# Expert stage of a fused attention and mixture-of-experts kernel: next unit's weights loaded ahead of row gathers, static weights moved to another queue, output tiles of their own

## The chip, the cores and the metric

The kernel runs on one core of one Trainium2 chip. The metric is the device time of one execution in microseconds (us). Three runs of the kernel before gave 756.05, 757.34 and 758.69 us, the median is 757.34 us. Engines are named as in the profile: PE (TensorE), PEld (its weight loads), DVE (VectorE), ACT (ScalarE), POOL (GpSimd) and SP (SyncE, which only issues DMAs here).

## What is computed

```
attn = clustered attention of q, k, v            # 2 x 8 heads x 768 x 64
x    = prelu(attn @ w_in) @ w_out                # 1536 tokens x 512, hidden 2048
do   = (x @ w_skip) > 0                          # tokens that go to an expert
e    = argmax(x @ w_gate, 8 experts)
gate = softmax(x @ w_gate)[e]
out  = x;  out[do] = x + gate * (relu(x @ w1[e]) @ w2[e])    # w1 512 x 1024, w2 1024 x 512
```

The change is in the last stage, the experts, and in the routing just ahead of it.

## The kernel before

The order of the instructions on each engine is written out by hand (a manual schedule). Attention and the dense layer fill the first 540 us. What follows is the expert stage, `moe2` (L1166), with the end of the routing, `route_last` (L1025), woven in.

**Units and tiles.** The stage has ten units, `TURNS = "01U2UZUVWV"`. A unit is one expert's weights and one or two tiles of tokens: units 0, 1 and 3 (the letters "0", "1", "2") have an expert that is known when the kernel is built, the others one that the routing picks. The sixteen tiles are t0 to t15: unit 0 has t0 and t1, unit 1 has t2, unit 2 has t3 and t4, unit 3 has t5, unit 4 has t6 and t7, unit 5 t8, unit 6 t9 and t10, unit 7 t11 and t12, unit 8 t13, unit 9 t14 and t15.

**Weights.** A unit's weights come in four chunks (c = 0 to 3) of 128x2048 float32, 1 MB each. `loadw(n, c)` (L1180) loads chunk c of unit n into a landing buffer, `raw` for odd units, `even` for even ones: for a unit with a picked expert by an indirect DMA that POOL issues (L1186) with row numbers `wi`, for a static one by a plain DMA from SP (L1184). `ahead()` in `run` then splits a chunk into a rounded high part, `wsp.hi` on ACT (L1432), and a low part, `wsp.lo` on DVE (L1436), and calls `loadw(n + 2, c)`. PE multiplies by both parts.

**Tiles.** `gather(t)` (L1174) is an indirect DMA from POOL that brings 128 token rows (L1163), with row numbers `gi`; `transx` turns them on PE, `first` is the first product, `transh` turns its result, `second` is the second product, `output(t)` (L1266) adds the gated result to the gathered rows `x` in place (DVE, L1278), and `scatter(t)` (L1281) writes them with an indirect DMA from POOL (L1283). A tile of x is kept in one of seven buffers, `XG = (1, 6)`, so `gather(t + 7)`, which stands right behind `scatter(t)` in the program, writes the buffer that `scatter(t)` reads. Each scatter waits for the one before it, since all write the same output.

**Routing.** `route_last` is a generator that `begin` (L1286) steps through between products. It makes `gi` from the product `sv` (L1118), `wi` and `si` from the product `eu` (L1135), and ends with the number of units, `nt`. Its tiles lie in a pool (`rwk`) that is closed after its end; the six buffers for gathered rows from t3 on (`moxg`) take that place.

**Queues.** POOL issues gathers, indirect weight loads and scatters in program order, and an instruction that waits holds all behind it. SP has a queue of its own.

Of the kernel before, what the change touches and what calls it, by code (L numbers as in the profile page):

```python
# [8 lines left out]
F32 = mybir.dt.float32  # L9
# [7 lines left out]
ALU = mybir.AluOpType  # L17
# [3 lines left out]
P = 128  # L21
# [5 lines left out]
DM = H * D  # L27
BIG = float(2 ** 60)
DFF = 2048
NE = 8  # L30
DE = 1024
NTT = N // P
NPC = 4
# [51 lines left out]
XG = (1, 6)  # L85
# [932 lines left out]
def route_last(nc, A, cst, R, wk, ps, yb, y1d):  # L1018
# [20 lines left out]
    s = wk.tile([P, KD, P], F32, tag="yts", name="yts")  # L1039
# [23 lines left out]
    def small(*shape):  # L1063
        return wk.tile([P, *shape], F32, name=f"rs{len(sizes)}", tag=f"rs{sizes.append(0) or len(sizes)}")
    sizes = []
    tm, cmp, m, nu, rem, n4, lim = small(NE), small(NE, 28), small(NE), small(NE), small(NE), small(4), small(3, 4)
    dist, far, bl, tri = small(3), small(3, NE), small(NE), small(4, NE, NE + 1)
    mt, sl4, ta, tb, sl = small(NTT, 4, NE), small(NTT, 4), small(NTT), small(NTT), small(NTT)
    tt, red = ve.tensor_tensor, ve.tensor_reduce
    steps = [  # L1070
        lambda: tt(out=tm, in0=rk[:, nt], in1=R["one8"][:, 1], op=ALU.max),
# [26 lines left out]
    more = positions(nc, R, wk, rk[:, :nt], t0, nt)  # L1098
# [18 lines left out]
    for i in range(NTT):  # L1117
# [5 lines left out]
    t2 = wk.tile([P, NTT, nx], F16, tag="t2", name="t2")  # L1123
    tt(out=t2, in0=sl.unsqueeze(2).to_broadcast([P, NTT, nx]),
       in1=R["first"].unsqueeze(1).to_broadcast([P, NTT, nx]), op=ALU.is_equal)
    es = wk.tile([P, NTT, NE], F32, tag="es", name="es")
    e0 = wk.tile([P, NTT], F32, tag="e0", name="e0")
    ve.tensor_tensor(out=es, in0=M, in1=R["e512"].unsqueeze(1).to_broadcast([P, NTT, NE]), op=ALU.mult)
    ve.tensor_reduce(out=e0, in_=es, axis=AX.X, op=ALU.add)
# [33 lines left out]
    nc.gpsimd.indirect_dma_start(out=x, out_offset=None, in_=y1d, in_offset=bass.IndirectOffsetOnAxis(ap=at, axis=0))  # L1163


def moe2(ctx, tc, A, cst, R, y1d, wsp, wk, ps, x0, route, room):  # L1166
    nc = tc.nc
    ident = cst["ident"]
    KD = DM // P
# [4 lines left out]
    def gather(t):  # L1174

        a, b = XG
        x = (wk if (t - 2) % (a + b) < a else more[0]).tile([P, DM + 1], F32, tag="xg", name="xg", bufs=a if (t - 2) % (a + b) < a else b)
        gather_rows(nc, x, y1d, R["gi"][:, t:t + 1])
        xg[t] = x

    def loadw(n, c):
        if n not in TOLD:
            r = (EXPERT[int(TURNS[n])] * NPC + c) * P
            nc.sync.dma_start(out=wsp.src(n, c), in_=A["wall"][r:r + P])  # L1184
            return
        nc.gpsimd.indirect_dma_start(out=wsp.src(n, c), out_offset=None, in_=A["wall"],  # L1186
                                     in_offset=bass.IndirectOffsetOnAxis(ap=R["wi"][:, TOLD[n], c:c + 1], axis=0),
                                     bounds_check=NE * NPC * P - 1, oob_is_err=False)
# [75 lines left out]
        scatter(t, output(t))  # L1264

    def output(t):  # L1266
        x = xg.pop(t)
        n, b0, nr = TILES[t]

        rows = slice(0, b0 + nr)  # L1270
        y = yo.pop(t)
        if is_half(t):
            o = wk.tile([P, DM], F32, tag="o", name="o", bufs=1)
            for r in range(b0, -1, -HALF):
                nc.scalar.copy(o[r:r + HALF], y[HALF - r:P - r])
            nc.vector.tensor_tensor(out=o[rows], in0=y[rows], in1=o[rows], op=ALU.add)
            y = o
        nc.vector.scalar_tensor_tensor(out=x[rows, :DM], in0=y[rows], scalar=x[rows, DM:DM + 1], in1=x[rows, :DM], op0=ALU.mult, op1=ALU.add)  # L1278
        return x

    def scatter(t, o):  # L1281
        rows = slice(0, TILES[t][1] + TILES[t][2])
        nc.gpsimd.indirect_dma_start(out=A["out"], out_offset=bass.IndirectOffsetOnAxis(ap=R["si"][rows, t:t + 1], axis=0), in_=o[rows, :DM], in_offset=None,  # L1283
                                     bounds_check=N - 1, oob_is_err=False)

    def begin():  # L1286

        low = []
        next(route)
        first(0, 0, range(0, 1))  # L1290
        wsp.take(1, 0)
        wsp.hi(1, 0)
        next(route)
        first(0, 0, range(1, 4))
        next(route)
        first(1, 0)
        transh(0, 0, low)
        first(0, 1)
        transh(1, 0, low)
        first(1, 1)  # L1300
        transh(0, 1, low)
        second(0, 0, (0,))
        next(route)
        gather(2)
        next(route)
        second(0, 0, (1,))
        wsp.take(1, 1)
        wsp.hi(1, 1)
        while low:
            low.pop(0)()  # L1310
        second(0, 1, (0,))
        next(route)
        transh(1, 1)
        for _ in route:
            pass
        more.append(room())
        for t in (3, 4):
            gather(t)
        for c in range(NPC):
            loadw(2, c)  # L1320
        second(0, 1, (1,))
        second(0, 0, (2,))
        wsp.lo(1, 0, nc.vector)
        wsp.take(1, 2)
        wsp.hi(1, 2)
        transx(2)
        second(0, 1, (2,))
        second(1, 0)
        wsp.lo(1, 1, nc.vector)
        scatter(0, output(0))  # L1330
        second(1, 1)
        wsp.lo(1, 2, nc.vector)
        scatter(1, output(1))
        for c in range(3):
            loadw(3, c)
        for t in range(5, sum(XG) + 2):
            gather(t)

    def run(n0, n1, fresh=False):

# [99 lines left out]
def kernel(ctx, tc, A):  # L1440
    nc = tc.nc
# [25 lines left out]
    R = {}  # L1467
# [177 lines left out]
    xg, (y, xT) = got  # L1645
    c3.close()
    c0.close()
    c4 = ctx.enter_context(ExitStack())
    rwk = c4.enter_context(tc.tile_pool(name="rwk", bufs=1, side="right", reuse_waits="tile"))
    yb = rwk.tile([P, DM], F32, name="yb")  # L1650
# [14 lines left out]
        c4.close()  # L1665
        return ctx.enter_context(tc.tile_pool(name="moxg", bufs=1, side="right", reuse_waits="tile"))

    moe2(ctx, tc, A, cst, R, y1d, wsp, mwk, ps, (xg, xT), route_last(nc, A, cst, R, rwk, ps, yb, y1d), room)


# [45 lines left out]
```

## Time and profile before

| | |
|---|---|
| median of 3 runs | 757.34 us (756.05 to 758.69) |
| the profiled execution's own time | 755.56 us |
| its span in the profile | 753.8 us |
| mean granted clock of PE in it | 0.978 |
| busy PE / PEld | 713.6 us (95%) / 628.3 us (83%) |
| busy DVE / ACT / POOL | 568.2 us (75%) / 477.7 us (63%) / 363.6 us (48%) |
| DMA | 109.22 MB, mean 145 GB/s |

Busy shares are means over the whole span; stages differ. In a row of the timeline the columns are: start in us from the span's start, duration in us, engine, line of the kernel, operation, output<-inputs, how many instructions were merged, and in brackets the idle time of that engine just before with what ended it ("issue": nothing that the profile shows). The time of the profiled execution stands 1.78 us under the median.

### The profile page before, as it was taken

How to read it: one execution, taken by the hardware profiler on the slowest of the kernel's cores; microseconds unless marked ns; L12 is line 12 of the kernel's file. 1: busy time of each engine (PE TensorE's matmuls, PEld its weight loads, DVE VectorE, ACT ScalarE, POOL GpSimd, SP SyncE). 2: the span in 40 equal slices, each digit the busy share in tenths (PEclk: the TensorE clock that was granted, in tenths of full speed). 3: DMA queues.
4: the chain of work that ended last, by engine and by line, in shares of the span. 5: the costliest groups of instructions: out<-in, count | busy, mean ns of one | idle time of the engine just before them, and what ended most of it. 6: DMA issues, size and time to landing. Idle time of an engine off the chain costs nothing. (4 is left out here: it accounts for less than half of the span.)

```text
span 753.8 us, 11621 instructions
## 1 busy us (share of the span) xinstructions
PE 713.6 (95%) x4022; PEld 628.3 (83%) x4022; DVE 568.2 (75%) x1110; ACT 477.7 (63%) x916; POOL 363.6 (48%) x336
## 2 busy tenths in 40 slices
PE   8999999999999999999999999999986999987993
PEld 5988998889998889888899999988875888876772
DVE  5989988898989788888759899764785677755641
ACT  5879889798899845554446555565445675645630
POOL 4649779788785576666640000010271565534311
PEclk8999999999999999999999999999996999999997
DMA  7867668574763324333126000355366674646600
GB/s 205 223 163 179 129 137 212 125 184 99 210 137 96 113 65 150 122 113 111 57 98 196 0 1 1 68 185 172 109 234 275 223 283 160 258 161 250 244 26 25
DMA packets 46161, 109.22 MB, mean 145 GB/s; under 512 B 10778, under 2 KB 26586, under 8 KB 40720
## 3 DMA queue, kind: packets, MB, share of 16 engines
q1 hardware_dynamic: 39600, 72.01, 34.7%
q0 software_dynamic: 6496, 36.40, 13.3%
q8 instruction: 34, 0.56, 0.3%
q14 instruction: 31, 0.25, 0.1%
HBM read 74.78 MB, written 10.10 MB: 113 GB/s over the span
## 5 line engine op out<-in xcount | busy, mean ns | idle before, releaser
L341 DVE TENSOR_TENSOR etl<-pt,eth 128x384 fp32r<-128x384 f32 x192 | 102.1, 550 | 20.5 <-ACT eth L340 18.9
L1163 POOL DMA_INDIRECT xg<-y1d,gi x16 | 22.9, 1430 | 176.7 <-DVE gi L1014 113.8
L340 ACT CAST eth<-pt 128x384 fp32r<-128x384 f32 x192 | 91.1, 487 | 20.4 <-PE pt L338 20.3
L338 PE MATMUL pt<-ident,e 128*128 128x128 f32 x576 | 93.8, 272 | 0.3 <-ACT e L327 0.3
L320 DVE TENSOR_REDUCE nm<-s 128x1 f32<-128x768 f32 x96 | 90.5, 944 | 4.0 <-PE s L307 3.8
L327 ACT ACTIVATE e<-s,nm 128x768 f32<-128x768 f32 x96 | 87.5, 911 | 5.8 <-DVE nm L320 5.1
L695 ACT CAST gh<-gm 128x384 fp32r<-128x384 f32 x60 | 30.8, 514 | 82.0 <-DVE gm L693 58.5
L338 PEld LDWEIGHTS pt<-ident,e 128*128 128x128 f32 x576 | 73.5, 140 | 7.1 <-ACT e L327 0.5
L697 DVE TENSOR_TENSOR gl<-gm,gh 128x384 fp32r<-128x384 f32 x60 | 49.4, 823 | 25.7 <-ACT gh L695 25.7
L1436 DVE TENSOR_TENSOR wl<-raw,wh 128x2048 fp32r<-128x2048 f32 (+2 forms) x27 | 46.6, 1735 | 28.9 <-ACT wh L1432 28.4
L356 PE MATMUL px<-etl,vh 128*64 128x384 f32 (+1 forms) x192 | 65.6, 369 | 1.7 <-DVE etl L341 1.5
L304 PE MATMUL s<-AB 128*128 128x384 f32 x192 | 57.6, 381 | 2.6 <-ACT e L327 2.0
L1432 ACT CAST wh<-raw 128x2048 fp32r<-128x2048 f32 (+2 forms) x27 | 39.3, 1462 | 27.5 <-DMA raw<-in_wall_dram,wi 20.0
L667 PE MATMUL h<-xh,wh 128*128 128x384 f32 x256 | 55.6, 338 | 0.6 <-DVE gm L690 0.4
L667 PE MATMUL h<-xh,wl 128*128 128x384 f32 x256 | 56.0, 340 | 0.0
L667 PE MATMUL h<-xl,wh 128*128 128x384 f32 x256 | 55.0, 336 | 0.0
L567 POOL TENSOR_TENSOR pre<-ct,pre 128x512 int32<-128x512 int32 x26 | 37.1, 1448 | 35.9 <-DVE ct L565 35.9
L358 PE MATMUL px<-eth,vh 128*128 128x384 f32 x160 | 54.0, 337 | 0.0
L307 PE MATMUL s<-CD 128*128 128x384 f32 x192 | 49.4, 338 | 0.9 <-DMA CD<-st 0.9
L667 PEld LDWEIGHTS h<-xh,wh 128*128 128x128 f32 x256 | 45.6, 188 | 3.3 <-DVE gm L690 0.5
L1283 POOL DMA_INDIRECT out_dram<-xg,si x16 | 20.8, 1302 | 54.0 <-issue 27.1
L667 PEld LDWEIGHTS h<-xh,wl 128*128 128x128 f32 x256 | 44.6, 188 | 2.7 <-POOL wl L639 2.6
(343 smaller groups left out, 1844.3 us busy)
## 6 DMA issues: line engine op xcount, KB each, us to landing
AB<-RL SPq DMA_DIRECT2D x32, 384.0 KB, 5.2
raw<-in_wall_dram SPq DMA_DIRECT2D x12, 1024.0 KB, 8.9
raw<-in_w_in_dram SPq DMA_DIRECT2D x16, 512.0 KB, 4.0
raw<-in_w_out_dram SPq DMA_DIRECT2D x16, 512.0 KB, 4.7
Tp<-in_qkT_dram SPq DMA_DIRECT2D x16, 384.0 KB, 3.8
CD<-RL SPq DMA_DIRECT2D x16, 384.0 KB, 6.6
vt<-in_v_dram SPq DMA_DIRECT2D x8, 384.0 KB, 6.2
y1d<-yb SPq DMA_DIRECT2D x12, 256.0 KB, 4.5
```

Of the source, the lines that this page charges most:

```text
L304: nc.tensor.matmul(s[:, u, :384], lhsT=AB[:, 0, t * P:(t + 1) * P], rhs=AB[:, 1, ks], start=True, stop=False)
L307: nc.tensor.matmul(s[:, u, :384], lhsT=CD[:, 0, t * P:(t + 1) * P], rhs=CD[:, 1, ks], start=False, stop=True)
L320: nc.vector.tensor_reduce(out=nm, in_=s[:, :, :384], axis=AX.XY, op=ALU.max, negate=True)
L327: nc.scalar.activation(e.rearrange("p (u c) -> p u c", u=2), s[:, :, :384], AF.Exp, bias=nm, accum_out=den[:, i % 3:i % 3 + 1])
L338: nc.tensor.transpose(pt[:, i2], e[:, kt * P:(kt + 1) * P], ident)
L340: nc.scalar.copy(eh, pt)
L341: lows[u] = lambda: nc.vector.tensor_tensor(out=etl[:, 3 * u:3 * u + 3, q * P:(q + 1) * P], in0=pt, in1=eh.bitcast(F32), op=ALU.subtract)
L356: nc.tensor.matmul(px[:m], lhsT=vh[:, kt, :m], rhs=etl[:, kt], start=False, stop=False)
L358: nc.tensor.matmul(px, lhsT=vh[:, kt, :], rhs=eth[:, kt], start=False, stop=(kt == NT - 1))
L667: nc.tensor.matmul(hs[c], lhsT=a[:, k * P:(k + 1) * P], rhs=x[:, k, c * HC:(c + 1) * HC], start=(k == 0 and i == 0), stop=(k == KD - 1 and ...
L697: eng.tensor_tensor(out=gl[:, o], in0=m, in1=gh[:, o].bitcast(F32), op=ALU.subtract)
L1436: eng.tensor_tensor(out=lo[:, a:b], in0=self.src(t, c)[:, a:b], in1=hi[:, a:b].bitcast(F32), op=ALU.subtract)
```

## The change

It makes five edits.

1. In `begin`, the loads of unit 2's chunks 0 and 1 are issued as soon as `wi` is there, ahead of the gathers of t3 and t4; chunks 2 and 3 follow after the gather of t3, and the gather of t4 comes behind them.
2. The static loads that `loadw` makes, the four chunks of unit 3, are issued by POOL and no longer by SP, and three of them are placed behind the gathers of t5 to t8; the fourth follows in `run`.
3. `output` writes into a tile of its own, `o` (two buffers in a new pool `moo`), which `scatter` reads; before it wrote into `x`. The pool also takes the one gather buffer that lay in `mowk`.
4. The step of `route_last` that makes `sv` and `gi` is called two groups of matmuls sooner.
5. Two temporaries of the routing (`mt`, `es`) take the room of a tile that is no longer read.

```diff
-    mt, sl4, ta, tb, sl = small(NTT, 4, NE), small(NTT, 4), small(NTT), small(NTT), small(NTT)
+    room = s.rearrange("p k m -> p (k m)")
+    mt = room[:, :NTT * 4 * NE].rearrange("p (t c e) -> p t c e", t=NTT, c=4)
+    sl4, ta, tb, sl = small(NTT, 4), small(NTT), small(NTT), small(NTT)
...
     def loadw(n, c):
         if n not in TOLD:
             r = (EXPERT[int(TURNS[n])] * NPC + c) * P
-            nc.sync.dma_start(out=wsp.src(n, c), in_=A["wall"][r:r + P])
+            nc.gpsimd.dma_start(out=wsp.src(n, c), in_=A["wall"][r:r + P])
             return
...
     def output(t):
+        o = op.tile([P, DM], F32, tag="o", name="o")
         x = xg.pop(t)
...
         if is_half(t):
-            o = wk.tile([P, DM], F32, tag="o", name="o", bufs=1)
             for r in range(b0, -1, -HALF):
...
-        nc.vector.scalar_tensor_tensor(out=x[rows, :DM], in0=y[rows], scalar=x[rows, DM:DM + 1], in1=x[rows, :DM], op0=ALU.mult, op1=ALU.add)
-        return x
+        nc.vector.scalar_tensor_tensor(out=o[rows], in0=y[rows], scalar=x[rows, DM:DM + 1], in1=x[rows, :DM], op0=ALU.mult, op1=ALU.add)
+        return o
...
         first(1, 1)
+        next(route)
         transh(0, 1, low)
         second(0, 0, (0,))
-        next(route)
         gather(2)
...
         transh(1, 1)
+        for c in range(2):
+            loadw(2, c)
         for _ in route:
             pass
         more.append(room())
-        for t in (3, 4):
-            gather(t)
-        for c in range(NPC):
-            loadw(2, c)
+        gather(3)
...
         transx(2)
+        for c in range(2, NPC):
+            loadw(2, c)
+        gather(4)
...
         scatter(1, output(1))
+        for t in range(5, sum(XG) + 2):
+            gather(t)
         for c in range(3):
             loadw(3, c)
-        for t in range(5, sum(XG) + 2):
-            gather(t)
...
+    mop = ctx.enter_context(tc.tile_pool(name="moo", bufs=2, side="right", reuse_waits="tile"))
```

POOL's queue at the start of the expert stage, before. `xg<-` are gathers, `even<-` the four chunks of unit 2, then of unit 4, `out_dram<-` scatters; the first row is routing.

```order
L1000 TENSOR_SCALAR poh<-iota,pos,tok_5478 128x128 x6
L1163 DMA xg<-y1d,gi 128x513 x3
L1186 DMA even_5272<-in_wall_dram,wi 128x2048
L1186 DMA even_6291<-in_wall_dram,wi 128x2048
L1186 DMA even_6539<-in_wall_dram,wi 128x2048
L1186 DMA even_6540<-in_wall_dram,wi 128x2048
L1283 DMA out_dram<-xg_3831,si 1536x512
L1283 DMA out_dram<-xg_3832,si 1536x512
L1163 DMA xg<-y1d,gi 128x513 x4
L1186 DMA even_5272<-in_wall_dram,wi 128x2048
```

The same place in the change; `raw<-in_wall_dram` without `wi` are the four static chunks of unit 3.

```order
L1165 DMA xg<-y1d,gi 128x513
L1188 DMA even_5272<-in_wall_dram,wi 128x2048
L1188 DMA even_6291<-in_wall_dram,wi 128x2048
L1165 DMA xg<-y1d,gi 128x513
L1188 DMA even_6542<-in_wall_dram,wi 128x2048
L1188 DMA even_6543<-in_wall_dram,wi 128x2048
L1165 DMA xg<-y1d,gi 128x513
L1285 DMA out_dram<-o,si 1536x512 x2
L1165 DMA xg<-y1d,gi 128x513 x4
L1186 DMA raw_78<-in_wall_dram 128x2048
L1186 DMA raw_79<-in_wall_dram 128x2048
L1186 DMA raw_3822<-in_wall_dram 128x2048
```

Unit 2's first two chunks moved from the fourth and fifth DMA of the stage to the second and third; t4's gather moved from third to sixth; four loads joined the queue behind the gathers of t5 to t8.

POOL's queue around the scatters of t2 to t4 and the gathers behind them, before, with what each waits for (DMASW: an earlier DMA of POOL's queue, DMAHW: one of SP's).

```order
L1283 DMA out_dram<-xg,si 1536x512 [waits DMASW2_49,DVE_49]
L1163 DMA xg<-y1d,gi 128x513 [waits DMASW3_49,DMASW2_49,PE_49]
L1186 DMA even_6540<-in_wall_dram,wi 128x2048 [waits DMASW4_49,DVE_49]
L1186 DMA raw_78<-in_wall_dram,wi 128x2048 [waits DMAHW3_49,DMASW5_49,DVE_49]
L1186 DMA raw_79<-in_wall_dram,wi 128x2048 [waits DMAHW4_49,DMASW6_49,DVE_49]
L1186 DMA even_5272<-in_wall_dram,wi 128x2048 [waits DMASW7_49,DVE_49]
L1186 DMA raw_3822<-in_wall_dram,wi 128x2048 [waits DMAHW5_49,DMASW0_49,DVE_49]
L1283 DMA out_dram<-xg,si 1536x512 [waits DMASW1_49,DVE_49]
L1163 DMA xg<-y1d,gi 128x513 [waits DMASW1_49,PE_49]
L1283 DMA out_dram<-xg,si 1536x512 [waits DMASW3_49,DVE_49]
L1163 DMA xg<-y1d,gi 128x513 [waits DMASW4_49,DMASW3_49,PE_49]
```

The same place in the change.

```order
L1285 DMA out_dram<-o,si 1536x512 [waits DMASW6_49,DVE_49,Activation_49]
L1165 DMA xg<-y1d,gi 128x513 [waits DMASW7_49,PE_49]
L1188 DMA even_6543<-in_wall_dram,wi 128x2048 [waits DMASW0_49,DVE_49]
L1188 DMA raw_78<-in_wall_dram,wi 128x2048 [waits DMASW1_49,DVE_49]
L1188 DMA raw_79<-in_wall_dram,wi 128x2048 [waits DMASW2_49,DVE_49]
L1188 DMA even_5272<-in_wall_dram,wi 128x2048 [waits DMASW3_49,DVE_49]
L1188 DMA raw_3822<-in_wall_dram,wi 128x2048 [waits DMASW4_49,DVE_49]
L1285 DMA out_dram<-o,si 1536x512 [waits DMASW6_49,DMASW5_49,DVE_49]
L1165 DMA xg<-y1d,gi 128x513 [waits PE_49]
L1285 DMA out_dram<-o,si 1536x512 [waits DMASW7_49,DMASW5_49,DVE_49]
L1165 DMA xg<-y1d,gi 128x513 [waits DMASW0_49,PE_49]
```

The order is the same; a gather behind a scatter waited for that scatter's DMA (DMASW2, DMASW1, DMASW3) and no longer does, while the second of two scatters still waits for the first.

DVE's output additions of t9 and t10 and what stands behind them, before.

```order
L1436 TENSOR_TENSOR wl_6290<-even_6540,wh_6289 128x2048 [waits DMASW6_49,Activation_49]
L1278 SCALAR_TENSOR_TENSOR xg<-yo,xg 128x512 [waits PE_49] x2
L1436 TENSOR_TENSOR lastl<-raw_78,lasth 128x2048 [waits DMASW7_49,Activation_49]
L1248 TENSOR_TENSOR hTl<-pt,hTh 128x512 [waits Activation_49]
L1436 TENSOR_TENSOR wl_5614<-raw_79,wh_5613 128x2048 [waits DMASW0_49,Activation_49]
```

The same place in the change.

```order
L1440 TENSOR_TENSOR wl_6290<-even_6543,wh_6289 128x2048 [waits DMASW2_49,Activation_49]
L1280 SCALAR_TENSOR_TENSOR o<-yo,xg 128x512 [waits DMASW6_49,DVE_49,PE_49]
L1280 SCALAR_TENSOR_TENSOR o<-yo,xg 128x512 [waits DMASW1_49,DVE_49,PE_49]
L1440 TENSOR_TENSOR lastl<-raw_78,lasth 128x2048 [waits DMASW3_49,Activation_49]
L1250 TENSOR_TENSOR hTl<-pt,hTh 128x512 [waits Activation_49]
```

The additions now wait for the scatter of two tiles earlier (DMASW6, DMASW1), whose buffer they write; the low parts of weights and activations stand behind them.

## Rows read from the trace of the kernel before

**Rows 1.** Busy time by stretch, all engines: stretch, length, busy time (instructions), PEclk, DMA share, GB/s.
```profile
565.00:570.00 5.00, 0.00 (x0) 0.00 (x0) 1.11 (x1) 3.04 (x4) 0.18 (x1) 0.73 1.01 428
575.00:580.00 5.00, 4.07 (x14) 3.40 (x14) 2.38 (x3) 2.17 (x2) 0.04 (x1) 0.50 0.47 188
...
620.00:640.00 20.00, 20.00 (x96) 16.40 (x95) 15.34 (x12) 11.79 (x13) 10.64 (x7) 1.00 0.49 171
...
680.00:700.00 20.00, 15.85 (x77) 13.14 (x77) 10.23 (x9) 9.61 (x11) 8.89 (x9) 0.91 0.72 276
```

**Rows 2.** Timeline, PE, around unit 1's end and in unit 2.
```profile
562.31 0.61 PE L1150 MATMUL pt<-ident,xg 128*128 128x128 f32 x4
571.57 2.07 PE L1195 MATMUL yo<-wh,hTh 128*128 128x512 f32 x4 [8.65 <-DVE hTh L1245]
...
590.08 0.60 PE L1240 MATMUL pt<-ident,hb 128*128 128x128 f32 x4
```

**Rows 3.** Timeline, ACT, the same stretch.
```profile
561.03 0.58 ACT L1151 CAST xTh<-pt 128x512 fp32r<-128x512 f32 x1
566.96 1.90 ACT L1432 CAST lasth<-even 128x2048 fp32r<-128x2048 f32 x1 [5.35 <-DMA even<-in_wall_dram,wi]
...
587.10 0.60 ACT L1224 ACTIVATE hb<-h 128x512 f32<-128x512 f32 x1 [0.21 <-PE h L1195]
...
597.87 1.91 ACT L1432 CAST wh<-even 128x2048 fp32r<-128x2048 f32 x1 [2.95 <-DMA even<-in_wall_dram,wi]
```

**Rows 4.** Timeline, POOL, the same stretch: gather, weight load, two scatters, weight load.
```profile
552.35 2.48 POOL L1163 DMA_INDIRECT xg<-y1d,gi  x1 [2.37 <-DVE nt L1145]
555.13 2.31 POOL L1186 DMA_INDIRECT even<-in_wall_dram,wi  x1 [0.30 <-issue]
...
564.15 1.02 POOL L1283 DMA_INDIRECT out_dram<-xg,si  x1 [0.31 <-issue]
579.96 2.40 POOL L1283 DMA_INDIRECT out_dram<-xg,si  x1 [14.78 <-issue]
...
590.33 2.88 POOL L1186 DMA_INDIRECT even<-in_wall_dram,wi  x1 [0.30 <-issue]
```

**Rows 5.** Timeline, SP's queue, the four static loads of unit 3.
```profile
554.07 9.27 SPq L1184 DMA_DIRECT2D raw<-in_wall_dram  x4
```

**Rows 6.** Timeline, DVE, the same stretch: wi, then low parts of weights.
```profile
549.95 0.22 DVE L1138 TENSOR_TENSOR wi<-et,prow 128x64 uint32<-128x64 f32 x1
...
551.71 2.29 DVE L1436 TENSOR_TENSOR wl<-raw,wh 128x2048 fp32r<-128x2048 f32 x1
...
560.71 2.28 DVE L1436 TENSOR_TENSOR wl<-raw,wh 128x2048 fp32r<-128x2048 f32 x1
...
568.89 2.29 DVE L1436 TENSOR_TENSOR lastl<-even,lasth 128x2048 fp32r<-128x2048 f32 x1 [5.29 <-ACT lasth L1432]
```

**Rows 7.** Timeline, PE, its gaps between 655 and 705 us and two pairs of transposes.
```profile
661.41 0.66 PE L1240 MATMUL pt<-ident,hb 128*128 128x128 f32 x4 [2.28 <-ACT hb L1224]
...
664.66 0.60 PE L1240 MATMUL pt<-ident,hb 128*128 128x128 f32 x4
...
666.17 0.66 PE L1157 MATMUL pt<-ident,xg 128*128 128x128 f32 x4 [0.47 <-DVE hTl L1248]
...
687.09 1.12 PE L1240 MATMUL pt<-ident,hb 128*128 128x128 f32 x4 [4.15 <-ACT hb L1224]
...
691.80 1.00 PE L1236 MATMUL pt<-two,hb 128*128 128x64 f32 x8
...
704.76 1.20 PE L1195 MATMUL yo<-wh,hTh 128*128 128x512 f32 x4 [0.87 <-DVE hTh L1245]
```

**Rows 8.** Timeline, ACT, its longest wait in that stretch.
```profile
682.84 1.90 ACT L1432 CAST wh<-raw 128x2048 fp32r<-128x2048 f32 x1 [12.21 <-DMA raw<-in_wall_dram,wi]
```

**Rows 9.** Timeline, POOL, a gather behind a scatter, and the load that ACT waited for.
```profile
668.49 0.98 POOL L1163 DMA_INDIRECT xg<-y1d,gi  x1 [8.35 <-DMA out_dram<-xg,si]
...
677.00 1.01 POOL L1186 DMA_INDIRECT raw<-in_wall_dram,wi  x1 [0.30 <-issue]
```

More of the change, by code (lines that the diff above doesn't have):

```diff
@@ L1125, in route_last @@
        in1=R["first"].unsqueeze(1).to_broadcast([P, NTT, nx]), op=ALU.is_equal)
-    es = wk.tile([P, NTT, NE], F32, tag="es", name="es")
+    es = room[:, NTT * 4 * NE:NTT * 5 * NE].rearrange("p (t e) -> p t e", t=NTT)
     e0 = wk.tile([P, NTT], F32, tag="e0", name="e0")
@@ L1163, in gather_rows, with moe2 @@
     nc.gpsimd.indirect_dma_start(out=x, out_offset=None, in_=y1d, in_offset=bass.IndirectOffsetOnAxis(ap=at, axis=0))
-def moe2(ctx, tc, A, cst, R, y1d, wsp, wk, ps, x0, route, room):
+def moe2(ctx, tc, A, cst, R, y1d, wsp, wk, op, ps, x0, route, room):
     nc = tc.nc
@@ L1176, in gather @@
         a, b = XG
-        x = (wk if (t - 2) % (a + b) < a else more[0]).tile([P, DM + 1], F32, tag="xg", name="xg", bufs=a if (t - 2) % (a + b) < a else b)
+        x = (op if (t - 2) % (a + b) < a else more[0]).tile([P, DM + 1], F32, tag="xg", name="xg", bufs=a if (t - 2) % (a + b) < a else b)
         gather_rows(nc, x, y1d, R["gi"][:, t:t + 1])
@@ L1277, in output @@
             y = o
-        nc.vector.scalar_tensor_tensor(out=x[rows, :DM], in0=y[rows], scalar=x[rows, DM:DM + 1], in1=x[rows, :DM], op0=ALU.mult, op1=ALU.add)
-        return x
+        nc.vector.scalar_tensor_tensor(out=o[rows], in0=y[rows], scalar=x[rows, DM:DM + 1], in1=x[rows, :DM], op0=ALU.mult, op1=ALU.add)
+        return o
     def scatter(t, o):
         rows = slice(0, TILES[t][1] + TILES[t][2])
-        nc.gpsimd.indirect_dma_start(out=A["out"], out_offset=bass.IndirectOffsetOnAxis(ap=R["si"][rows, t:t + 1], axis=0), in_=o[rows, :DM], in_offset=None,
+        nc.gpsimd.indirect_dma_start(out=A["out"], out_offset=bass.IndirectOffsetOnAxis(ap=R["si"][rows, t:t + 1], axis=0), in_=o[rows], in_offset=None,
                                      bounds_check=N - 1, oob_is_err=False)
@@ L1666, in room @@
         return ctx.enter_context(tc.tile_pool(name="moxg", bufs=1, side="right", reuse_waits="tile"))
-    moe2(ctx, tc, A, cst, R, y1d, wsp, mwk, ps, (xg, xT), route_last(nc, A, cst, R, rwk, ps, yb, y1d), room)
+    moe2(ctx, tc, A, cst, R, y1d, wsp, mwk, mop, ps, (xg, xT), route_last(nc, A, cst, R, rwk, ps, yb, y1d), room)
 _OUTS = [((N, DM), 'float32')]
```

## The prediction

> **What bounds the kernel now.** I read the page first (PE busy 95% of the span), then busy time by stretch, then PE's timeline where it was idle, and from there the timelines of whoever it waited for. In the expert stage PE is the bound wherever its input is there: 20.00 of 20 us from 620 to 640, but nothing from 565 to 570 and 15.85 of 20 from 680 to 700 [rows 1]. So time can come from PE's gaps and from what the granted clock does around them, and from nothing else.
>
> There are two sets of gaps. The first is 8.65 us up to 571.57 [rows 2]. Its chain: PE waits for a low part of activations on DVE, which stands behind the low part of a weight chunk (568.89) [rows 6], which waits for ACT's cast of that chunk at 566.96, and the cast waited 5.35 us for the DMA [rows 3]. The chunk is unit 2's first, issued at 555.13 [rows 4], so it took 11.8 us to land. In that time the DMA engines were full (share 1.01, 428 GB/s from 565 to 570 [rows 1]): SP had started unit 3's four static megabytes at 554.07 [rows 5], which nobody needs yet. The granted clock fell in the gap (0.73 over 565 to 570, then 0.50, the lower of the two levels, 1.2 of 2.4 GHz) and was still 0.50 from 575 to 580 [rows 1].
>
> The second set is 2.28, 0.47, 4.15 and 0.87 us between 661 and 705, 7.77 us in all [rows 7]. They are one story: weights come late because POOL issues them late. ACT waited 12.21 us for a chunk [rows 8] that POOL issued only at 677.00, after gathers had held its queue; the gather at 668.49 sat 8.35 us until the scatter's DMA released its buffer [rows 9]. Five gathers in the stage wait like that, 7 to 9 us each.
>
> **The change part by part.**
>
> *Routing product sooner.* The same matmuls in another order, in a stretch where PE was not idle: 0 us, between a loss of 0.6 (one transposition, if PE must now wait for DVE) and a gain of nothing, since t2's rows were not waited for. The moved temporaries change no duration: 0.
>
> *Unit 2's chunks first.* `wi` is ready at 550.17 [rows 6]. An issue takes 1.02 us and 0.30 between two; beside a low part of weights on DVE it takes more, 2.48 for the one at 552.35, which ended 0.83 us after the low part that ran until 554.00 [rows 4, 6]. Landing comes 4.7 us after an issue's end (593.21 to 597.87) [rows 3, 4]. Chunk 0 is therefore issued at about 550.5 and lands at 556, far ahead of 561.6, when ACT is free for it (561.03 + 0.58) [rows 3]. The cast ends at 563.5, the low part runs from 563.6 to 565.9, and PE could go on 2.68 us after that start, as before (568.89 to 571.57), at 566.3 instead of 571.57 [rows 2, 6].
>
> *But t4's gather is late.* It is now sixth in POOL's queue. Ahead of it four DMAs pass beside the low parts that DVE runs from 551.71 to 562.99 [rows 6], so it is issued by 561.5 to 564 and lands 4.7 us later, at 566.2 to 568.7. PE transposes it (0.61, at 562.31 before [rows 2]) ahead of the product that ends the gap. PE goes on at 566.8 to 569.3; I take 567.5, a gap of 4.6 us.
>
> *Static loads behind thirteen other DMAs.* This takes back most of that gain. The scatter of t1 waits for that of t0: 14.78 us before, behind full DMA engines [rows 4]; now less is queued, and I put it at 567.5 (t0's scatter issued at 562 to 564, its data landing no later than 4.7 us after). Before, from that scatter to the first load behind the four gathers took 10.37 us (579.96 to 590.33) and the landing another 7.54 (to 597.87) [rows 3, 4]. The same pattern puts unit 3's first chunk in place at 585.4. ACT's cast of it (1.90) stands ahead of the `hb` of t4 (0.60, at 587.10 before [rows 3]), which PE transposes at 590.08 [rows 2]. PE would get there at 583.5: from 567.5, the 18.5 us of before (571.57 to 590.08) less some 2.5 for matmuls no longer at 0.50 (an estimate; PE was busy 4.07 of 5 us at that clock in one stretch of the two [rows 1]). The chunk lets it go on at 585.4 + 1.90 + 0.60 = 587.9. So a gap of 4.4 us opens, and what is left of the 8.65 is 590.08 - 587.9 = **2.2 us**. A plain load issued by POOL has no row; I price it as an indirect one of the same size. If t1's scatter goes at 566.9 and all issues are undisturbed, the chunk lands at 579.2, PE never waits and 7.3 us are gained; if the scatter goes at 570.5, the chunk lands at 588.4 and 0.8 us are lost.
>
> *The clock.* After the 2.28 us gap the three groups up to the next transposition took 3.25 us (661.41 to 664.66), after the 4.15 us gap 4.71 (687.09 to 691.80) [rows 7], where the granted clock was 0.91 over the stretch [rows 1]: 1.46 us more. I take that loss for a gap of 4.4: **-1.46**. A like loss after the earlier gap would fall into the wait for the chunk and cost nothing.
>
> *Outputs in tiles of their own.* Same DVE instructions, same sizes. The gather behind a scatter waits for DVE's addition alone, long past, so the five waits of 7 to 9 us leave POOL's queue, and what comes next is DVE's low part of the chunk whose buffer a load reuses. Unit 7's chunks are then issued some 20 us sooner than they were (an estimate, from two to three such waits); they were late by at most 12.21 [rows 8]. The whole second set goes, with the clock loss after it: **7.77 + 1.46 = 9.2 us**; nothing if POOL stays as late as now. What is late next is nothing: PE's work from 655 to 705 is what it was full with from 620 to 640. Against that the additions wait for the scatter two tiles earlier (third rival).
>
> *Sum:* 2.2 - 1.46 + 9.2 = 10.0 us. The profiled execution took 755.56 us (span 753.8) and becomes 745.6; it stands 1.8 under the median, so the median goes from 757.34 to **747.3 us**.
>
> **The rivals.**
>
> *Unit 3's chunks come in time* (17%). Then 7.3 + 9.2 = 16.5 us, 740.8 us. For it: several of POOL's issues may miss the low parts and take 1.02. Against: before, in the like stretch, most met one.
>
> *The second set of gaps stays, in part or whole* (12%). A second scatter of a unit still waits for the first, and loads stand behind both: 14.78 us was one such wait [rows 4]. With half the 9.2 the median is 752.0 us; with none 756.6, no change.
>
> *Two output buffers, full queue: slower* (8%). All of POOL's DMAs now share one queue. Before t2's scatter stand seven chunks. At 428 GB/s [rows 1] one takes 2.45 us, so from 583 they end at about 600 and the scatter lands at 602; t4's addition, which needs that buffer, comes near 604. The margin is under 2 us. If a plain load from POOL moves at half that rate, unit 3's second chunk is 4.9 us late and the scatter 9.8; DVE then stands some 8 us with low parts behind it, of which 4 to 5 reach PE, and again at t5: 2.2 - 4.9 - 1.46 - 9 + 9.2 = -4 us, 761 us. It decides from about one and a half times 2.45 us a chunk. The Trainium skill has a rule that speaks for this rival: DMA: Bandwidth & Descriptors, section SWDGE vs HWDGE vs iDMA, sends plain transfers to SP or ACT and leaves GpSimd the irregular ones, since GpSimd's descriptors are written by software and VectorE can lock it out while it does so. The lengthened issue at 552.35 agrees with the lock; that a chunk moves more slowly for it no row shows, and the one landing behind a 2.88 us issue speaks against [rows 3, 4].
>
> **How the numbers follow.** The forecast has 55% (745 to 750.5, by where the chunk lands), the rivals 17, 12 and 8, the remaining 8% small mixtures of them. The range 740.5 to 753.5 us takes in the first rival and half of the second, and leaves out the third. About 0.3% (2.3 us) is what a measurement of this kernel can tell from no change. Faster by more than that: 55 + 17 + some 6 of the second rival + 7 = 85%; within it 7%; slower 8%.
>
> **What would show it.** Right: unit 2's first chunk landed before ACT asks; PE's first gap down to 4 or 5 us, ended by a gather or by DVE; a new gap of 3 to 6 us in unit 2, ended by `hb`, with ACT waiting for a `raw` load without `wi`; POOL's gathers behind scatters without waits; no PE gap from a late chunk after 600. Wrong: if the new gap is missing (first rival), if ACT still waits for indirect `raw` loads in units 7 to 9 (second), or if additions on DVE or copies on ACT wait for scatters (third).

## The result and the profile after

| | before | after |
|---|---|---|
| median, measured side by side | 756.11 us (754.07 to 758.69) | 742.95 us (742.39 to 743.77) |
| the profiled execution's own time | 755.56 us | 742.98 us |
| its span | 753.8 us | 741.2 us |
| busy PE | 713.6 us (95%) | 711.5 us (96%) |

The ratio is 0.9825, 95% interval 0.9805 to 0.9845: faster by 13.2 us where 10.0 were forecast. PE runs the same 4022 matmul instructions; of the 12.6 us that the span lost, 10.5 are PE's idle time and 2.1 its busy time (the mean granted clock is 0.985 where it was 0.978).

The second set of gaps [rows 7] is gone. Busy time by stretch in the changed kernel (columns as in rows 1):

```profile
560.00:565.00 5.00, 4.16 (x15) 3.48 (x16) 4.31 (x4) 3.39 (x5) 3.03 (x2) 0.66 0.95 377
565.00:570.00 5.00, 4.08 (x27) 3.48 (x26) 2.67 (x4) 3.25 (x5) 1.73 (x2) 1.00 0.12 48
570.00:575.00 5.00, 2.66 (x6) 2.17 (x7) 4.48 (x3) 2.10 (x2) 4.39 (x3) 0.68 0.43 112
...
585.00:590.00 5.00, 3.50 (x19) 2.96 (x20) 4.02 (x3) 4.71 (x6) 4.39 (x3) 1.00 1.01 428
...
680.00:700.00 20.00, 20.00 (x104) 16.68 (x104) 14.02 (x13) 12.12 (x14) 4.34 (x3) 1.00 0.09 30
```

PE is now full from 680 to 700 where it had 15.85 of 20, and the DMA share is 0.09 where it was 0.72 [rows 1]: the weights have long been there. POOL's timeline says why: a gather right behind a scatter, its next weight loads, and a second scatter of a unit:

```profile
662.65 0.99 POOL L1165 DMA_INDIRECT xg<-y1d,gi  x1 [0.30 <-issue]
663.95 2.10 POOL L1188 DMA_INDIRECT raw<-in_wall_dram,wi  x1 [0.31 <-issue]
...
681.88 1.01 POOL L1285 DMA_INDIRECT out_dram<-o,si  x1 [8.67 <-issue]
```

The gather no longer waits for a scatter's DMA (8.35 us in [rows 9]). A second scatter of a unit still waits 7 to 9 us for the first, but what stands behind it is not yet needed.

The first set of gaps, one of 8.65 us [rows 2], has become four small ones. PE's timeline:

```profile
560.84 0.66 PE L1152 MATMUL pt<-ident,xg 128*128 128x128 f32 x4 [1.86 <-DMA xg<-y1d,gi]
...
566.57 0.63 PE L1152 MATMUL pt<-ident,xg 128*128 128x128 f32 x4 [0.81 <-DMA xg<-y1d,gi]
...
572.34 2.08 PE L1197 MATMUL yo<-wh,hTh 128*128 128x512 f32 x4 [2.44 <-DVE hTh L1247]
...
586.50 0.66 PE L1242 MATMUL pt<-ident,hb 128*128 128x128 f32 x4 [1.89 <-ACT hb L1226]
...
589.75 0.60 PE L1242 MATMUL pt<-ident,hb 128*128 128x128 f32 x4
```

The first two wait for the gathers of t3 and t4, the third for a low part, the fourth for unit 3's first static chunk. ACT's casts of unit 2's first chunk and of that static chunk:

```profile
562.01 1.90 ACT L1436 CAST lasth<-even 128x2048 fp32r<-128x2048 f32 x1
...
584.05 1.90 ACT L1436 CAST wh<-raw 128x2048 fp32r<-128x2048 f32 x1 [4.62 <-DMA raw<-in_wall_dram]
```

Unit 2's chunk was there before ACT asked (5.35 us of waiting before [rows 3]). The static chunk is now what ACT waits for. POOL's queue from unit 2's first chunk on, without the rows between:

```profile
549.93 1.03 POOL L1188 DMA_INDIRECT even<-in_wall_dram,wi  x1 [2.24 <-DVE sk L1142]
551.26 1.00 POOL L1188 DMA_INDIRECT even<-in_wall_dram,wi  x1 [0.30 <-issue]
552.57 1.94 POOL L1165 DMA_INDIRECT xg<-y1d,gi  x1 [0.30 <-ACT wh L1436]
...
560.23 1.06 POOL L1165 DMA_INDIRECT xg<-y1d,gi  x1 [0.30 <-issue]
...
567.97 1.00 POOL L1285 DMA_INDIRECT out_dram<-o,si  x1 [4.41 <-ACT xTh L1153]
...
576.56 2.22 POOL L1186 DMA_DIRECT2D raw<-in_wall_dram  x4
```

By unit 2's second transposition of `hb` the changed kernel is 590.08 - 586.50 = 3.58 us ahead; the profiled executions differ by 755.56 - 742.98 = 12.58, so 9.0 us come after it. Of the 3.58, 0.20 stood before any edited code: PE's transposition of `hb` at 539.35 before is at 539.15 here. Two executions of the same code can be further apart than that (e1, e5 below), so a trace is read from such a common row on.

### The profile page after: what moved, and what is told of

It reads as the page before. It is cut to its first block, busy times and chain, and to the rows that moved or that the text cites. A ratio compares the mean times of both kernels' runs of the same rounds, so it can differ in the third digit from the quotient of the medians.

```text
span 741.2 us, 11633 instructions
## 1 busy us (share of the span) xinstructions
PE 711.5 (96%) x4022; PEld 628.5 (85%) x4022; DVE 567.2 (77%) x1110; ACT 478.4 (65%) x916; POOL 367.2 (50%) x340
## 5 line engine op out<-in xcount | busy, mean ns | idle before, releaser
L1165 POOL DMA_INDIRECT xg<-y1d,gi x16 | 21.4, 1338 | 130.1 <-DVE gi L1014 113.8
L1285 POOL DMA_INDIRECT out_dram<-o,si x16 | 18.6, 1162 | 73.4 <-DVE o L1280 39.5
```

## The experiments

The theory: the two sets are separate. Output tiles bring the 9 us after 600; the order of POOL's queue brings the rest, and there each wait that goes uncovers the next transfer. The main rivals were that the order of the loads brings the whole gain and that the queue of the static loads doesn't matter. The medians, each beside the kernel before on the same chip (its median there lay between 754.38 and 756.23 us, so small differences between rows are better read from the ratios):

| kernel | median (range), us | ratio to before (95%) |
|---|---|---|
| e1: output tiles alone | 745.74 (742.43 to 747.68) | 0.9888 (0.9862 to 0.9915) |
| e2: the change, outputs in place | 752.36 (750.40 to 756.49) | 0.9959 (0.9934 to 0.9985) |
| e3: the change, static loads from SP | 749.37 (748.35 to 750.09) | 0.9927 (0.9902 to 0.9951) |
| e4: the change, old order of gathers and chunks | 747.57 (746.08 to 748.39) | 0.9901 (0.9875 to 0.9927) |
| e5: the change, `sv` late again | 744.84 (744.60 to 748.96) | 0.9877 (0.9854 to 0.9900) |
| e6: gathers between chunks | 746.20 (745.16 to 747.32) | 0.9884 (0.9865 to 0.9903) |
| e7: e6 and static chunks sooner | 745.34 (742.51 to 745.56) | 0.9872 (0.9854 to 0.9890) |
| e8: static chunks sooner | 743.67 (741.57 to 744.30) | 0.9848 (0.9828 to 0.9869) |
| e0: the change again | 742.17 (741.19 to 743.82) | 0.9836 (0.9807 to 0.9866) |
| e9: low parts behind `hTh` | 740.62 (739.88 to 744.82) | 0.9823 (0.9791 to 0.9856) |
| e10: e7 and low parts behind `hTh` | 746.03 (743.37 to 746.58) | 0.9878 (0.9848 to 0.9908) |
| e11: e8 and low parts behind `hTh` | 742.70 (740.79 to 744.41) | 0.9840 (0.9810 to 0.9870) |

**e1, output tiles alone.** Edits 3 and 5 on the kernel before; orders, queue and `sv` as they were.

```diff
+        o = op.tile([P, DM], F32, tag="o", name="o")
         x = xg.pop(t)
```

> The kernel before with the output tiles alone (edits 3 and 5); order of loads, static loads on SP and the routing product as before. Theory (the late gaps of PE between 655 and 705 us come from gathers that wait for scatters, so the output tiles alone remove them): 9.2 to 9.5 us less than before, about 746.5 us; the first gap of 8.65 us is still there, PE is full from 600 to 720 us. Rival (the late gaps went because the loads of units 2 and 3 were put earlier, which moved POOL's whole queue forward): within 2 us of before, late gaps as before.

745.74 us, as the theory had it. PE's first gap stays as it was, and the late ones are gone (timeline of PE, then busy time by stretch):

```profile
570.08 2.08 PE L1197 MATMUL yo<-wh,hTh 128*128 128x512 f32 x4 [8.72 <-DVE hTh L1247]
...
586.32 0.60 PE L1242 MATMUL pt<-ident,hb 128*128 128x128 f32 x4
```
```profile
660.00:680.00 20.00, 20.00 (x96) 16.36 (x94) 11.67 (x11) 10.77 (x12) 14.56 (x10) 1.00 0.97 379
680.00:700.00 20.00, 20.00 (x104) 16.67 (x104) 14.02 (x13) 12.12 (x14) 5.70 (x3) 1.00 0.26 99
```

The tiles alone are worth 1.1% (0.85 to 1.38), some 8.5 us, or 10.5 by the medians. The trace agrees, read with care, for it is of the shortest of the four executions (742.43 us, as short as the change's). At unit 2's second transposition, 586.32, it is 3.76 us ahead of the kernel before with the first gap untouched: 1.57 us stood before the edited code (the row of 539.35 is at 537.78), and the granted clock read 1.00 from 575 to 580 where it was 0.50 [rows 1]. The other 9.4 us of its 13.1 come after that point.

**e2, all but the tiles.**

```diff
-        o = op.tile([P, DM], F32, tag="o", name="o")
...
-        return o
+        return x
```

> The changed kernel with outputs written in place into the gathered rows again (edit 3 undone, all else changed). Theory: only the first set of gaps stays improved, the late ones come back in part or whole since gathers wait for scatters again: 748 to 753 us. Rival (queue moved forward is enough): 743 to 745 us, PE full after 600 us.

752.36 us, 9.4 above the change. The gaps are back (PE), behind a late chunk (ACT) and a gather that waited for a scatter (POOL):

```profile
656.85 0.66 PE L1242 MATMUL pt<-ident,hb 128*128 128x128 f32 x4 [1.46 <-ACT hb L1226]
...
680.75 0.66 PE L1242 MATMUL pt<-ident,hb 128*128 128x128 f32 x4 [1.74 <-ACT hb L1226]
...
699.13 1.20 PE L1197 MATMUL yo<-wh,hTh 128*128 128x512 f32 x4 [3.00 <-DVE hTh L1247]
```
```profile
676.49 1.90 ACT L1436 CAST wh<-raw 128x2048 fp32r<-128x2048 f32 x1 [9.91 <-DMA raw<-in_wall_dram,wi]
```
```profile
600.56 0.98 POOL L1165 DMA_INDIRECT xg<-y1d,gi  x1 [14.78 <-issue]
```

With e1 this shows from both sides that the second set of gaps belongs to edit 3.

**e3, the queue of the static loads.**

```diff
-            nc.gpsimd.dma_start(out=wsp.src(n, c), in_=A["wall"][r:r + P])
+            nc.sync.dma_start(out=wsp.src(n, c), in_=A["wall"][r:r + P])
```

> The changed kernel with the static loads of unit 3 issued by SP again, all else changed. Theory (moving them to POOL is worth something because they leave the DMA engines to unit 2): the loads start near 554 us again, the gathers of t3 and t4 land later by 2 to 4 us, PE's first gaps grow by as much, the gap before unit 2's second tile (1.89 us) goes: 743 to 746 us. Rival (order alone does it, the queue is of no account): 741 to 743 us.

749.37 us, 6.4 above the change: the direction was right, the size missed. SP starts the four static megabytes at once, and the gathers land late (SP's queue, then PE); the gap before unit 2's second tile is gone, as expected:

```profile
554.78 9.27 SPq L1186 DMA_DIRECT2D raw<-in_wall_dram  x4
```
```profile
563.22 0.66 PE L1152 MATMUL pt<-ident,xg 128*128 128x128 f32 x4 [3.20 <-DMA xg<-y1d,gi]
...
575.60 1.09 PE L1152 MATMUL pt<-ident,xg 128*128 128x128 f32 x4 [7.46 <-DMA xg<-y1d,gi]
```

**e4, the old order** (gathers of t3 and t4, then unit 2's four chunks), the rest as in the change.

```diff
-        for c in range(2):
-            loadw(2, c)
         for _ in route:
...
-        gather(3)
+        for t in (3, 4):
+            gather(t)
+        for c in range(NPC):
+            loadw(2, c)
...
-        for c in range(2, NPC):
-            loadw(2, c)
-        gather(4)
```

> The changed kernel with unit 2's four chunks behind the gathers of t3 and t4, as before (edit 1 undone); static loads stay on POOL. Theory (the competition of the static loads, not the order, made the first chunk late): the chunk is issued near 555 us, lands near 562 us, hardly later than ACT asks, and the gathers are not late: 742 to 744 us. Rival (the order is what matters): the first gap is 5 us or more, 745 to 748 us.

747.57 us: the rival's number by another way than the rival's. Chunk 0 landed 0.33 us after ACT was free for it (the theory's point), but PE then stood at the static chunk (PE, then ACT):

```profile
565.56 2.07 PE L1197 MATMUL yo<-wh,hTh 128*128 128x512 f32 x4 [3.69 <-DVE hTh L1247]
...
589.11 1.11 PE L1242 MATMUL pt<-ident,hb 128*128 128x128 f32 x4 [7.24 <-ACT hb L1226]
```
```profile
586.66 1.90 ACT L1434 CAST wh<-raw 128x2048 fp32r<-128x2048 f32 x1 [9.96 <-DMA raw<-in_wall_dram]
```

Order and queue seem to work only together: old order with SP 745.7 (e1), old with POOL 747.6 (e4), new with SP 749.4 (e3), new with POOL 743.0. With the old order POOL is no better than SP (the intervals of e1 and e4 overlap); with the new one it is 6.4 us better. The four are not a clean square, though: e1 also has edit 4 undone, and the old order with SP and an early `sv` was not run.

**e5, edit 4 undone.**

```diff
-        next(route)
         transh(0, 1, low)
         second(0, 0, (0,))
+        next(route)
         gather(2)
```

> The change with its edit 4 undone: the slot numbers' product stands two matmul groups later again, all else as in the change. My theory: in the change the product ended 0.34 us sooner on the path (PE stood at 551.88 where it stood at 552.22 before), and POOL's first static gather of unit 2 had waited for the slot numbers (2.24 us for DVE's sk), so without the edit POOL's row of gathers and chunks starts some tenths to 2 us later, and the change has slack there of 0.9 to 1.9 us at its three small gaps: 743 to 744.5. Rival: those three gaps (1.86, 0.81 and 2.44 us) are ended by the gathers, so each microsecond by which POOL starts later is added to the first: 744.5 to 746.

744.84 us, between 1.9 and 2.7 us above the change by medians and 0.4 to 0.5% (3 to 4 us) by ratio, at and beyond the theory's upper end: the rival's number. No time of e5 is as short as any of the change's twelve (at most 743.82), but its interval touches that of e0, so the size is rough. Its profiled execution (747.23, one of the two long ones of six) shows POOL, DVE, and PE's second gap:

```profile
552.33 3.10 POOL L1188 DMA_INDIRECT even<-in_wall_dram,wi  x1 [0.30 <-issue]
...
562.50 1.88 POOL L1165 DMA_INDIRECT xg<-y1d,gi  x1 [0.30 <-PE pt L1152]
```
```profile
552.26 2.29 DVE L1440 TENSOR_TENSOR wl<-raw,wh 128x2048 fp32r<-128x2048 f32 x1
```
```profile
570.21 1.09 PE L1152 MATMUL pt<-ident,xg 128*128 128x128 f32 x4 [5.21 <-DMA xg<-y1d,gi]
```

The second chunk's issue, 1.00 us at 551.26 in the change, starts 1.07 us later, just behind the start of DVE's low part, and takes 3.10; it ends 0.88 us after that low part does (554.55). So 1.07 us of delay became 3.17, and PE's transposition of t4 came 3.64 later (570.21 against 566.57). In the change the low part began at:

```profile
551.38 2.29 DVE L1440 TENSOR_TENSOR wl<-raw,wh 128x2048 fp32r<-128x2048 f32 x1
```

0.12 us behind the issue that it would have held. Most of the 1.07 us is not the edit's. PE's transposition of `hb` ahead of the edited code, in the change and in e5:

```profile
539.15 0.60 PE L1242 MATMUL pt<-ident,hb 128*128 128x128 f32 x4
```
```profile
539.90 0.60 PE L1242 MATMUL pt<-ident,hb 128*128 128x128 f32 x4
```

0.75 us stood there already, so the edit moved the issue by some 0.3 us, from 0.12 ahead of the low part to 0.07 behind its start, and of t4's 3.64 us some 2.9 are its doing. Whether the issue was held in the four short executions too, no trace shows. The Trainium skill (SBUF — State Buffer, section SBUF: two separate sides) says that a DMA issued by GpSimd may have to wait until a VectorE operation lets go of a shared port, and gives some 115 ns behind that operation's end. The held issue agrees; the 0.88 us is longer.

**e6, e7, e8: the small gaps.** e6 issues gather t2, chunk 0, gather t3, chunk 1, gather t4, chunks 2 and 3:

```diff
-        for c in range(2):
-            loadw(2, c)
+        loadw(2, 0)
...
         gather(3)
+        loadw(2, 1)
+        gather(4)
...
-        gather(4)
```

e8 leaves the change's order and moves two static loads:

```diff
-        scatter(0, output(0))
+        o0 = output(0)
...
-        scatter(1, output(1))
+        o1 = output(1)
+        for c in range(2):
+            loadw(3, c)
+        scatter(0, o0)
+        scatter(1, o1)
...
-        for c in range(3):
-            loadw(3, c)
+        loadw(3, 2)
```

e7 does both.

> The change with POOL's order gather t2, chunk 0, gather t3, chunk 1, gather t4, chunks 2 and 3 (the change has both first chunks ahead of gather t3). My theory: the waits of 1.86 and 0.81 us that the gathers of t3 and t4 end go, chunk 1 still lands in time, but PE then comes sooner to unit 2's second transposition and the wait for unit 3's first static chunk there (1.89 us) grows by as much, as that chunk's issue stands behind the scatter of t1: 742 to 743.5, the change's own time or up to 1 us less. Rival: chunk 1 or the later ones come late in their turn and PE waits for them: 744 to 747. A second rival: the waits go and the static chunk moves forward with everything else, 740 to 741.5.

> The same order of gathers, and the loads of unit 3's static chunks 0 and 1 issued ahead of the scatters of t0 and t1. My theory: all three waits go (1.86 + 0.81 by the order, 1.89 by the static chunk), with some tenths given back to the queue: 738.5 to 741. Rival: the static chunks, issued sooner, share the DMA engines with unit 2's chunks 2 and 3 and the gathers, and one of those comes late by as much: 742 to 746.

> The change with only the loads of unit 3's static chunks 0 and 1 moved ahead of the scatters of t0 and t1. My theory: only the wait of 1.89 us at unit 2's second transposition goes: 740.5 to 741.7. Rival: the static chunks, issued sooner, take the DMA engines from unit 2's chunks and gather t4, which makes the waits of 0.81 and 2.44 us longer: 743 to 746.

None is faster than the change, and all three came out at their rivals' numbers; e8 can't be told from the change (the intervals overlap). In e6 the two gathers' waits are gone, and in their place stand (PE):

```profile
566.33 2.08 PE L1197 MATMUL yo<-wh,hTh 128*128 128x512 f32 x4 [3.26 <-DVE hTh L1247]
...
588.53 1.12 PE L1242 MATMUL pt<-ident,hb 128*128 128x128 f32 x4 [5.88 <-ACT hb L1226]
...
594.09 0.60 PE L1242 MATMUL pt<-ident,hb 128*128 128x128 f32 x4
```

t1's scatter went at 571.05 instead of 567.97 and the static loads behind it at 580.00 instead of 576.56, so what the theory named, the static chunk, is late by more than it said. e7's profiled execution has no gap over 0.93 us but one of 3.27, with the clock low behind it (last section), and no late chunk as its rival had it; but it is the shortest of the five, 742.51, as short as the change. The other four took 744.48 to 745.56, three of them at a higher mean clock (0.986 to 0.989) than the profiled one (0.980), so what lengthened them is not that clock loss and stays open. e8 removed the wait at the static chunk, as expected, but the waits for the gathers became 2.20 and 2.06 us, and one of 1.07 opened at 599.29.

**e0, e9, e10, e11: DVE's order, and the change once more.** In e9 the low parts of unit 2's chunks stand behind the low part of `hTh` on DVE (`low_load` makes the low part and issues the load of two units on, so those loads move with it):

```diff
             wsp.hi(n, c)
-            wsp.lo(n, c, nc.vector)
+            if n == 2:
+                later.append((n, c))
...
                 transh(*wait.pop(0))
+            while later:
+                low_load(*later.pop(0))
```

> The changed kernel itself, word for word, beside the next three: it gives the number that they are held against on the same chip. Expected 742.4 to 744.5, from its six times of 742.39 to 743.77.

> The change, with DVE's low parts of unit 2's four chunks emitted behind the low part of the transposed activations (hTh) instead of ahead of it. In the change PE waits 2.44 us at 572.34 for hTh, which stands on DVE behind the 2.29 us low part of a chunk. My theory: that wait falls below 1 us, but the wait for unit 3's first static chunk at unit 2's second transposition (1.89 us, chunk landed 584.05) grows by what is won, so the time stays within 1 us of the change; 742 to 744. Rival: the drop of the granted clock to 0.68 behind the 2.44 us wait goes with the wait and unit 3's chunk is no later bound: 739.5 to 741.5.

> Three edits together: gathers of t3 and t4 between unit 2's chunks, unit 3's static chunks 0 and 1 issued ahead of the scatters of t0 and t1, and the low parts behind hTh. The kernel with the first two had PE gaps of 3.27 (hTh behind a low part) and 0.93 us and no other up to 600, and the granted clock at 0.50 to 0.63 for some 10 us behind the first. My theory: the first gap falls to under 2 us (1.5 us sooner), the other stays; with the clock drop as it was 741 to 743.5, and without it, since the busy time at half speed there costs some 5.8 us, 736 to 739. Rival: chunks 2 and 3 or t4's gather come late in turn and it stays at 744 to 746.

> Two edits: static chunks 0 and 1 ahead of the scatters, low parts behind hTh, with the gathers in the order of the change. The kernel with the first alone has gaps of 2.20, 2.06, 0.93 and 1.07 us. My theory: the gathers' gaps of 2.20 and 2.06 stay since the transfers set them, and only the 0.93 goes: 742 to 744. Rival: the sooner low part moves the row of waits forward as a whole: 740 to 741.5.

e9 is 1.5 us below the change's 742.17 by the medians, at the rival's number, but the ranges overlap: a hint, not a result; four of its six times lie from 739.88 to 740.78. In its profiled execution, one of the two long ones (743.31), the 2.44 us gap is 0.93 and the wait at the static chunk is gone, against the theory, but the waits for the gathers are 2.65 and 2.94 us and the granted clock is 0.50 from 570 to 575, against the rival. e11 is as the change, at its theory's number, though the 0.93 us gap that was to go is still there. e10, with all edits that looked good, is slower, 746.03, by a chunk that neither its theory nor its rival had named. No gap of the first set is over 1.84 us there, the granted clock is 1.00 from 540 to 590, and then comes (ACT, then PE):

```profile
597.65 1.90 ACT L1449 CAST wh<-even 128x2048 fp32r<-128x2048 f32 x1 [11.28 <-DMA even<-in_wall_dram,wi]
```
```profile
600.08 2.08 PE L1197 MATMUL yo<-wh,hTh 128*128 128x512 f32 x4 [5.46 <-ACT hTh L1243]
```

That is unit 4's first chunk. In e10 the static loads ahead of t0's scatter delay its data, t1's scatter waits for that until 575.43 (567.97 in the change), and unit 4's chunk, behind it in POOL's queue, is issued at 587.45 instead of 579.09. In e6, e8 and e10 alike, what was brought forward made another transfer the late one.

## Why the prediction was right, and where it was not

The range of 740.5 to 753.5 us held the result, and both mechanisms were right in the main: the second set of gaps went with the output tiles, and of the first a wait for unit 3's static chunk took back a part. The number was less good: 742.95 us lies below the band of the forecast's main line (745 to 750.5), between it and the first rival (740.8), and a range 13 us wide is hard to miss. Of the 4.35 us between 747.3 and 742.95, 1.23 are the kernel before, at 756.11 beside the change and not 757.34; the rest is a gain of 13.2 for 10.0. By the steps:

- *Outputs in tiles of their own, 9.2 us.* Right: 9.0 us lie behind unit 2 in the traces, 9.4 between the change and e2, 8.5 to 10.5 in e1. The chunk for which ACT waited 12.21 us, issued at 677.00 before [rows 9], is issued at 649.74, 27 us sooner where some 20 were estimated. The second rival (the set stays in part) and the third (two buffers, slower) fell: PE is without a gap from 600 to 720, so no addition's wait for a scatter reached it.
- *Unit 2's chunks first.* Right in what happened: chunk 0 issued at 549.93 (550.5 was forecast), landed before ACT asked. The cause was in part another: e4 shows that it would land all but in time (0.33 us late) from the old place as well, once SP no longer loads beside it. I credited the order with what the queue alone does; what the order buys is that everything behind, down to the static loads, is issued some 4 us sooner.
- *t4's gather is late.* Half right: issued at 560.23, ahead of the 561.5 to 564 forecast; PE transposes t4 at 566.57, inside 566.2 to 568.7. But I missed t3: its gather stands behind two chunks, its issue ended at 554.51 and PE waited until 560.84, 6.3 us where I took 4.7. The gap of 4.6 us came as 1.86 + 0.81 + 2.44 = 5.1.
- *Static loads behind thirteen other DMAs.* Right in its mechanism: t1's scatter at 567.97 (567.5), a new gap ended by `hb`, ACT waiting for `raw` without `wi`. A term was mis-sized: the first load came 8.59 us behind that scatter, not 10.37. It landed 7.49 us after (7.54 forecast), at 584.05 instead of 585.4. PE also arrived later, at 584.61 and not 583.5, so the gap is 1.89 us, not 4.4. That the landing came so near is in part luck: it hangs in part on edit 4, which the forecast priced at nothing (in e5's long execution it is 588.25, of which 0.75 stood from the start).
- *The clock, -1.46.* This loss did not come: behind the 1.89 us gap the granted clock stayed at 1.00, and from that transposition to the next took 3.25 us (586.50 to 589.75), full speed by [rows 7]. It was priced for a gap of 4.4 us, and for longer gaps in that place it was of the right kind: behind 5.88 us in e6 the same stretch took 5.56 us (588.53 to 594.09), behind 7.24 us in e4 4.94 us (589.11 to 594.05). With the term before, that is the miss of the sum: 3.58 us at unit 2's second transposition where 2.2 - 1.46 = 0.7 was forecast, 1.4 by the static chunk and 1.46 by the clock.
- *A clock loss after the earlier gap costs nothing.* Right, though it fell into the wait for t4's gather and not, as forecast, into the one for the chunk; shown by chance. The second run of the change (e0) met the same gap at full clock. PE's timeline in e0, then in the change's first profile:

```profile
561.26 1.17 PE L1197 MATMUL h<-wh,xTh 128*128 128x512 f32 x4
562.28 1.09 PE L1197 MATMUL h<-wl,xTh 128*128 128x512 f32 x4
...
566.58 0.63 PE L1152 MATMUL pt<-ident,xg 128*128 128x128 f32 x4 [2.37 <-DMA xg<-y1d,gi]
```
```profile
561.25 1.76 PE L1197 MATMUL h<-wh,xTh 128*128 128x512 f32 x4
562.80 1.91 PE L1197 MATMUL h<-wl,xTh 128*128 128x512 f32 x4
```

  The next product waits for t4's gather and stands at 566.58 and 566.57. The executions took 742.86 and 742.98 us.
- *Routing product sooner, 0 us.* This failed: 2 to 4 us (e5), where a gain of nothing was the upper bound. The step looked at t2's rows alone, which nobody waits for, and not at the chunk loads, which edit 1 had just put right behind the slot numbers (POOL's 2.24 us wait for `sk` at 549.93). It is not a further term beside the sum: what it gives shows in when the gathers and the static loads land.
- *A plain load from POOL, priced as an indirect one.* Right: 7.49 us from issue to landing, with 428 GB/s moving from 585 to 590, where SP's four in e3 took 10.3 to 14.8 us beside the gathers, and no low part of DVE held the issue of a plain load (e8, last section). I gave the third rival, with slower loads, 8% and cited the Trainium skill beside it (DMA: Bandwidth & Descriptors, section SWDGE vs HWDGE vs iDMA). Read as a rule for the time, it would make e3 the faster kernel. e3 is 6.4 us slower: SP's loads start while the gathers are in flight. What the runs point to is when a load starts; the two engines with the same start were not compared.

That edits 1, 2 and 4 together are worth some 3 to 5 us follows from e1 and the change (2.8 by medians, 0.63% by ratio), not from a sum over e3, e4 and e5: each of these alone costs 2 to 6.4 us when undone, because the three share one queue.

## What to carry to other kernels

An in-place output couples the write-back to the next load of the same buffer; two small tiles that break this were worth some two thirds of the gain here. Put a load that nobody needs yet into the same queue behind the ones that are needed: the queue is then a priority list. The order of the rest has to suit it: with the old order (e4) the move brought nothing that e1 does not have. Once the waits are a few small ones with different releasers, moving one transfer forward delayed another here; such orders (e6 to e11) can be tried, but their sum is not the sum of the gaps they remove.

## What the runs showed of the hardware that I had not expected

- The length of a gap does not tell whether PE's granted clock falls behind it. In the change it read 0.66 over the stretch behind a gap of 1.86 us and 0.68 behind 2.44 us (0.50 is the lower level, 1.2 of 2.4 GHz), but 1.00 behind 1.89 us and, in e0, 1.00 behind 1.82 us at the same place in the program. e6 and e7 have the same gap, 3.26 and 3.27 us, ended at 566.33 and 566.23. Busy time by stretch, 565 to 575, in e6 and in e7:

```profile
565.00:570.00 5.00, 3.67 (x11) 2.95 (x11) 4.07 (x4) 1.66 (x1) 0.00 (x0) 0.66 0.62 226
570.00:575.00 5.00, 4.07 (x22) 3.36 (x21) 2.40 (x2) 3.29 (x5) 3.34 (x3) 1.00 0.21 65
```
```profile
565.00:570.00 5.00, 3.77 (x10) 3.01 (x10) 3.96 (x4) 1.54 (x1) 0.00 (x0) 0.50 0.99 367
570.00:575.00 5.00, 4.07 (x15) 3.40 (x14) 1.58 (x2) 2.17 (x2) 0.00 (x0) 0.50 0.67 264
```

  e7 stayed at the lower level through both stretches, e6 was back after the first. What decides between them stays open.
- Four plain loads of 1 MB are issued by POOL in 2.22 us together, 0.56 to 0.61 each; an indirect one takes 1.0 us undisturbed.
- An indirect POOL issue that begins within a low part of DVE ends 0.84 to 0.90 us after it, wherever in it it began (eight issues between 552 and 564 in the change and e5); one that begins 0.12 us ahead is not held (551.26 in the change). That is how a shift of 0.3 us at the start of a queue could be worth three. A plain load issued by POOL is not held: in e8 two stand wholly within a low part and take 1.18 us together, as they do elsewhere (e7, e10 and e11 show the same). POOL, then DVE, in e8:

```profile
561.64 1.18 POOL L1186 DMA_DIRECT2D raw<-in_wall_dram  x2
```
```profile
560.72 2.28 DVE L1443 TENSOR_TENSOR wl<-raw,wh 128x2048 fp32r<-128x2048 f32 x1
```

  The held issue does not explain all times that fall into two groups: in e9 (four from 739.88 to 740.78, two at 743.31 and 744.82) the profiled execution is a long one, and its second chunk's issue took 1.00 us. The two long ones have the lowest mean clock of the six (0.984 and 0.985 against 0.986 to 0.992); the cause was not tested.
